# Moving the seam between two instruction orders from word 571 to word 1042

## The chip, the cores and the metric

The kernel runs on one core of a Trainium2 chip. The metric is device time in microseconds, from one launch to its end; a run is told by its time, and a change by the medians of runs of both kernels on the same chip. The engines go by the short names of the profile: PE is TensorE (PEld its weight loads), DVE is VectorE, ACT is ScalarE, POOL is GpSimd and SP is SyncE, which issues most of the DMAs.

## The reference

Two blocks follow each other. The first is a linear attention with a complex, data-dependent decay (batch 4, 8 heads, 768 positions, head size 48). The second is a feed-forward block with three up-projections, of which the maximum is taken, and one down-projection.

```python
mag = np.sqrt(a_re * a_re + a_im * a_im)
scale = np.minimum(mag, 0.999) / (mag + 1e-06)
a_re_n, a_im_n = (a_re * scale, a_im * scale)
for t in range(S):                                  # S_re, S_im start at zero
    ar, ai = (a_re_n[:, :, t, :, None], a_im_n[:, :, t, :, None])
    new_re = ar * S_re - ai * S_im
    new_im = ar * S_im + ai * S_re
    kv = np.einsum('bhd,bhe->bhde', k[:, :, t], v[:, :, t])
    S_re, S_im = (new_re + kv, new_im)
    y[:, :, t] = np.einsum('bhd,bhde->bhe', q[:, :, t], S_re)
x = y.transpose(0, 2, 1, 3).reshape(3072, 384)
h = np.maximum(np.maximum(x @ w1, x @ w2), x @ w3)  # w1, w2, w3: 384 x 768
out = h @ w_out                                     # w_out: 768 x 384
```

All tensors are float32.

## The kernel before

The positions are cut into 24 tiles of 128 (4 batch rows of 6 tiles). Two tiles, called x and y, of two batch rows make one group, and there are 12 groups, 0 to 11. The work of a group is cut into some hundred and fifty short steps. Each step has a name and a group number, and such a pair is called a word: `Fy:6` is step `F` of tile y in group 6. The string `SCHEDULE` lists 1,880 words in one order, written out in full, and the kernel runs through it and emits each word's instructions. A small class wraps each engine and chains its instructions, so each engine runs its own words strictly in the order of the list; across engines the tile framework puts semaphores where data or buffers demand it.

```python
def g(*a, **kw):
    ins = f(*a, **kw)
    if self.last is not None:
        tc.add_manual_dep(ins.ins, self.last.ins.name, order, reason="the schedule's order")
```

The order in `SCHEDULE` is put together from two orders: words up to a seam come from one, and the rest, those not used yet, from the other, in its sequence. The seam stands at word 571.

Two more tables go with the list. `SLOTS` gives, for each PSUM tile in the order of its first use, one of four slots named 0, 2, 4 and 6, of two banks each; a tile has to wait until the last reader of the slot's tile before is done. `OTHER` names the words that run on the engine that is not their usual one: copies (`Kc`, `Qc`, `x`), magnitudes (`abs`, `af`) and maxima (`relu`, `u01`, `u11`) go from ACT to DVE, and the additions `Lnop` and `addw` go from a DMA issued by POOL to DVE.

```python
def banks(nm, n=None):
    ps = psum.tile([P, 2, 512], FP, tag="ps" + next(slots), name=nm)

def activation(func, **kw):
    need = SETS.get(func, T.get("set"))
    if need != T.get("set"):
        act.preload_act_table_set(need)
        T["set"] = need
    act.activation(func=func, **kw)
```

ACT has two sets of function tables, one for Ln and Exp and one for Sin and Arctan. `activation` puts a table load into ACT's queue whenever the set changes from one word to the next; copies, Relu, Abs and Square run with either set.

The words that matter below, with the engine of each:

- Gates, one word a group: `sqr`, `sqi`, `lnL`, `expw`, `expe`, `lne`, `relu`, `abs`, `lnw`, `expL`, `atan` on ACT, `add`, `xor`, `half`, `mulai`, `mulw`, `stt`, `turn` on DVE; `Lnop` and `addw` add by DMA. They turn `a_re`, `a_im` into a log magnitude `Ln` and an angle `w` (`expL` is an Exp, `atan` an Arctan).
- Angles, one word a tile: `cs` sums the angles on PE, `t` (ACT) and `nf` (DVE) take off whole turns, `Cd` carries the last angle into the next group's `ar` by two DMAs that POOL issues and that add, `sa` and `sb` are the Sin words on ACT.
- Decays: `sums` and `F` on PE; `En`, `Ek`, `Eq` and `f0` to `f3` are Exp words on ACT.
- Keys and queries: `mk`, `mq`, `uk`, `uq`, `kEn`, `Q1`, `Q2`, `KB`, `QB`, `QG` on DVE; `tpk`, `tpq` transpose on PE, `Kc`, `Qc` copy the result out of PSUM.
- Scores and state: `A`, `B`, `dk`, `y` on PE; `g0` to `g3` and `h0` to `h3` on DVE, `b0`, `b1` on ACT; `x` copies `y` out of PSUM into the features (`xy:5` is that copy for tile y of group 5).
- Feed-forward: `U01`, `U02`, `U11`, `U12` (nine products of 128 rows each) on PE, and `u` of the same number takes the maximum (`u01`, `u11` on ACT, `u02`, `u12` on DVE). The down-projection is done by Strassen's scheme: sums `S1` to `S4` on DVE, products `P1` to `P7`, `Px`, `Py` on PE, results `r1`, `r6`, `r75`, `r57`, `ox`, `oy` on ACT and DVE. `Dx`, `Dy` write the output.
- Loads: `Lr`, `Li`, `Lk`, `Lq`, `Lv`, all issued by SP.

PE works on pieces of its array that differ in shape. `U`, `P` use 128*128 (rows * columns), `A`, `B`, `y` 128*32, `cs` 128*64, `tpk`, `tpq` 64*128 and `sums`, `F`, `dk` 64*64. A tile change is two words in turn on PE with different shapes. All lines of the profile name line 201, the wrapper, so groups of instructions are told apart by tile.

Of the kernel before, what the change touches and what calls it, by code (L numbers as in the profile page):

```python
# [54 lines left out]
Cdy:3 Lkx:4 f1x:4 f0x:4 U01:2 uqy:3 f3x:4 mulw:4 stt:4 atan:4 tpky:3 Kcy:3 Ax:3 g0x:3 mqx:4 g1x:3 Bx:3 g2x:3 g3x:3 b1x:3
b0x:3 u01:2 Cdx:3 turn:4 U02:2 Lrx:5 u02:2 mkx:4 kEny:3 csy:4 csx:4 tx:4 nfx:4 ty:4 nfy:4 yx:3 xx:3 sumsy:4 KBy:3 Eqy:4
Eky:4 Lry:5 S3:2 Eny:4 sqr:5 dky:3 h1y:3 h2y:3 h3y:3 tpqy:3 Qcy:3 Q2y:3 Lix:5 sqi:5 Px:2 afy:4 add:5 lnL:5 expe:5 Dy:1
U12:2 u12:2 S1:2 Py:2 P7:2 Q1y:3 relu:5 lne:5 QBy:3 afx:4 P4:2 Ay:3 By:3 expw:5 S2:2 g0y:3 sbx:4 abs:5 g1y:3 sax:4 QGy:3
ukx:4 uqx:4 P6:2 P5:2 S4:2 g2y:3 g3y:3 P2:2 P1:2 Lqy:4 r1:2 Liy:6 mqy:4 b1y:3 P3:2 b0y:3 r6:2 r75:2 tpkx:4 r57:2 ox:2
# [5 lines left out]
sumsy:5 h1y:4 h2y:4 tx:5 nfx:5 h3y:4 afy:5 yx:4 Eky:5 Eny:5 Eqy:5 afx:5 Q2y:4 Q1y:4 sbx:5 P5:3 P1:3 P7:3 Lky:5 sax:5
Ay:4 xx:4 KBy:4 ukx:5 uqx:5 Lrx:7 tpqx:5 S2:3 expw:6 relu:6 QBy:4 Lnop:6 mky:5 tpkx:5 S4:3 Kcx:5 g0y:4 Qcx:5 P6:3 Px:3
Py:3 r1:3 By:4 P2:3 P4:3 say:5 sby:5 QGy:4 g1y:4 abs:6 g2y:4 g3y:4 b1y:4 b0y:4 KBx:5 mqy:5 r6:3 r75:3 r57:3 kEnx:5 oy:3
Q1x:5 uky:5 xor:6 Lry:7 sqr:7 Fy:5 f2y:5 sumsx:6 uqy:5 f3y:5 yy:4 P3:3 ox:3 f0y:5 Lkx:6 xy:4 QGx:5 addw:6 U11:4 Liy:7
Dx:3 QBx:5 Ekx:6 mkx:6 Enx:6 Lvx:5 f1y:5 lnw:6 Lqx:6 h0y:5 u11:4 Q2x:5 expL:6 mulai:6 mulw:6 U01:4 u01:4 tpky:5 h0x:5
# [10 lines left out]
tx:7 afy:7 yx:6 xx:6 Ay:6 S1:5 dky:6 h1y:6 nfx:7 h2y:6 h3y:6 Px:5 Py:5 abs:8 addw:8 half:8 g0y:6 g1y:6 say:7 KBy:6 sby:7  # L80
Lqy:7 P1:5 r1:5 g2y:6 afx:7 S2:5 P2:5 P7:5 sbx:7 sax:7 QBy:6 P5:5 lnw:8 ukx:7 S4:5 g3y:6 P6:5 mqy:7 r6:5 uqx:7 Lqx:8
QGy:6 P3:5 By:6 P4:5 r75:5 r57:5 tpkx:7 oy:5 ox:5 b0y:6 kEnx:7 mky:7 uky:7 b1y:6 tpqx:7 yy:6 Kcx:7 uqy:7 xy:6 expL:8
mulw:8 sumsx:8 Qcx:7 Eqx:8 mulai:8 mqx:8 Q1x:7 Ekx:8 Lkx:8 mkx:8 Fy:7 f1y:7 f0y:7 f3y:7 Enx:8 f2y:7 QGx:7 U01:6 Lvx:7
QBx:7 Q2x:7 u01:6 U11:6 Cdy:7 Liy:9 u11:6 Lvy:8 tpky:7 kEny:7 h0x:7 tpqy:7 Kcy:7 h0y:7 dkx:7 Qcy:7 sumsy:8 Fx:8 Eky:8
Eqy:8 h1x:7 Eny:8 h2x:7 KBx:7 f2x:8 f0x:8 h3x:7 Q2y:7 stt:8 Dx:5 f1x:8 atan:8 Cdx:7 turn:8 Lix:9 Lrx:9 Ax:7 g0x:7 g1x:7
Lry:9 sqr:9 Dy:5 g2x:7 sqi:9 add:9 f3x:8 lnL:9 expe:9 U12:6 lne:9 u12:6 Lvy:7 g3x:7 U02:6 u02:6 S3:6 Bx:7 b0x:7 b1x:7
dky:7 S1:6 h1y:7 h2y:7 csx:8 csy:8 tx:8 ty:8 nfy:8 h3y:7 afy:8 yx:7 xx:7 P7:6 relu:9 expw:9 KBy:7 say:8 sby:8 Lqy:8 P1:6
S2:6 P6:6 nfx:8 Q1y:7 QBy:7 Lky:8 mky:8 By:7 afx:8 uky:8 sbx:8 Ay:7 abs:9 Lnop:9 tpky:8 Lrx:10 QGy:7 g0y:7 g1y:7 g2y:7
sax:8 Kcy:8 P5:6 S4:6 g3y:7 ukx:8 r1:6 uqx:8 mqy:8 r6:6 h0x:8 b0y:7 r75:6 r57:6 b1y:7 Px:6 P2:6 P3:6 Py:6 P4:6 kEny:8
tpkx:8 ox:6 oy:6 addw:9 lnw:9 tpqx:8 yy:7 Qcx:8 sumsx:9 Kcx:8 kEnx:8 xy:7 Fy:8 Q1x:8 sumsy:9 Enx:9 xor:9 f1y:8 f0y:8  # L90
expL:9 half:9 mulai:9 Cdy:8 f2y:8 f3y:8 Eny:9 Liy:10 mulw:9 QGx:8 stt:9 U11:7 KBx:8 Eky:9 uqy:8 Lry:10 sqr:10 Lqx:9
Ekx:9 Lix:10 Lvx:8 sqi:10 Lkx:9 mkx:9 Eqx:9 QBx:8 u11:7 mqx:9 Q2x:8 U01:7 Cdx:8 atan:9 u01:7 add:10 lnL:10 Eqy:9 expe:10
U02:7 turn:9 tpqy:8 Qcy:8 dkx:8 relu:10 u02:7 h1x:8 Fx:9 Dy:6 h2x:8 Dx:6 f1x:9 f0x:9 Ax:8 h3x:8 Bx:8 g0x:8 g1x:8 U12:7
g2x:8 g3x:8 lne:10 Q2y:8 f3x:9 b0x:8 f2x:9 h0x:9 Lqy:9 Q1y:8 csy:9 ty:9 u12:7 S3:7 csx:9 nfy:9 expw:10 tx:9 b1x:8 S1:7
P1:7 r1:7 QBy:8 S2:7 nfx:9 KBy:8 sbx:9 afy:9 Ay:8 g0y:8 g1y:8 afx:9 g2y:8 g3y:8 Lky:9 yx:8 xx:8 sax:9 say:9 ukx:9 abs:10
By:8 h0y:8 sby:9 mky:9 P6:7 uqx:9 P7:7 mqy:9 P5:7 r6:7 S4:7 Py:7 b0y:8 Px:7 r75:7 r57:7 QGy:8 P4:7 oy:7 tpqx:9 tpkx:9
Lnop:10 Kcx:9 b1y:8 sumsx:10 kEnx:9 Qcx:9 Q1x:9 dky:8 h1y:8 h2y:8 h3y:8 Enx:10 uky:9 addw:10 lnw:10 Lkx:10 P2:7 expL:10
P3:7 Ekx:10 ox:7 KBx:9 yy:8 xy:8 Fy:9 f0y:9 f1y:9 QGx:9 f2y:9 Lvx:9 f3y:9 dkx:9 Eqx:10 QBx:9 U01:8 mkx:10 u01:8 Q2x:9
Ax:9 xor:10 half:10 h1x:9 Lvy:9 Bx:9 uqy:9 h2x:9 h3x:9 U11:8 g0x:9 Liy:11 g1x:9 Dy:7 g2x:9 g3x:9 Lqx:10 mqx:10 Cdy:9
u11:8 Fx:10 b0x:9 b1x:9 tpky:9 tpqy:9 kEny:9 Lry:11 mulw:10 mulai:10 stt:10 Dx:7 f1x:10 f3x:10 Qcy:9 Kcy:9 Q2y:9 U02:8  # L100
u02:8 f2x:10 U12:8 Lrx:11 sqr:11 Cdx:9 S3:8 atan:10 turn:10 f0x:10 Lix:11 yx:9 sqi:11 add:11 lnL:11 xx:9 expe:11 csy:10
xor:11 ty:10 csx:10 u12:8 S1:8 KBy:9 sumsy:10 nfy:10 Eny:10 Eky:10 S2:8 Q1y:9 QBy:9 afy:10 Eqy:10 Lqy:10 dky:9 P5:8
tx:10 lne:11 P6:8 P7:8 Ay:9 h0y:9 nfx:10 h1y:9 By:9 QGy:9 h2y:9 h3y:9 g0y:9 sbx:10 g1y:9 g2y:9 relu:11 afx:10 sax:10
ukx:10 g3y:9 P1:8 S4:8 r1:8 say:10 sby:10 mqy:10 r6:8 r75:8 b0y:9 b1y:9 expw:11 Py:8 P4:8 r57:8 Px:8 uqx:10 yy:9 xy:9
# [938 lines left out]
```

## Time and profile before

| What | Value |
|---|---|
| Time, median of 3 runs | 558.26 us (557.66 to 558.30) |
| The profiled execution | 555.38 us, its span 553.6 us |
| Granted PE clock, mean | 0.991 |
| Busy: PE, DVE, ACT, POOL | 525.3, 482.6, 365.0, 71.8 us |
| ACT table loads | 47, 1283 ns each |
| DMA | 47.90 MB, mean 87 GB/s |

The span goes from the first to the last instruction of the profiled execution; the time of that execution is 1.8 us longer. Busy times are unions over the span; PE's matmuls overlap each other, so a matmul's own duration (382 ns for the largest group) is longer than the time that one adds (the 792 of that group are busy for 177.4 us). From 110 to 495 us PE is busy at least 99% of every 55 us, and the first 55 us hold 35.75 us of PE work.

### The profile page before, as it was taken

The page shows a single profiled execution, that of the slowest core. Times are in us where ns is not written, and L with a number is a line of the kernel's source. Part 1 is how long each engine was busy: PE and PEld are TensorE (multiplying, and loading weights), DVE is VectorE, ACT ScalarE, POOL GpSimd, SP SyncE. Part 2 cuts the span into 40 slices and gives each one's busy share as a digit, 9 for nine tenths or more (in the row PEclk, how much of TensorE's full clock was granted, in tenths as well). Part 3 has the DMA queues.
Part 4 walks back from the last instruction along what each step waited for, and adds up shares of the span by engine and source line. Part 5 has one row for each costly group of instructions (what it writes and reads, how often), then busy time and mean ns, then how long its engine had stood idle before and what let it go on. Part 6 is the DMA issues. An engine that isn't in the chain of part 4 may idle for free.

```text
span 553.6 us, 22691 instructions
## 1 busy us (share of the span) xinstructions
PE 525.3 (95%) x10086; PEld 449.6 (81%) x10086; DVE 482.6 (87%) x752; ACT 365.0 (66%) x650; POOL 71.8 (13%) x114
## 2 busy tenths in 40 slices
...
GB/s 217 295 247 176 157 136 79 48 128 77 2 117 103 59 118 73 61 50 84 95 96 58 37 100 119 75 92 49 69 122 17 32 110 68 2 31 2 31 1 28
DMA packets 142097, 47.90 MB, mean 87 GB/s; under 512 B 130480, under 2 KB 135600, under 8 KB 142000
## 3 DMA queue, kind: packets, MB, share of 16 engines
...
q8 instruction: 79, 1.29, 1.0%
q14 instruction: 18, 0.15, 0.1%
...
## 4 chain that ended last, share of the span: by engine, by line
PE 84%; DVE 7%; ACT 4%; issue 2%; SPq 2%; DMA 1%; DVEq 0%; ACTq 0%
PE up L201 33%; PE op L201 24%; PE y L201 7%; PE A L201 5%; PE tp L201 4%; PE dk L201 3%; PE cs L201 3%; PE sums L201 2%; DVE w L201 2%; SPq L201 2%; PE F L201 2%; PE B L201 1%; DVE atm L201 1%; DMA wo<-in_moe_w_dram 1%; DVE uk L201 1%
## 5 line engine op out<-in xcount | busy, mean ns | idle before, releaser
L201 PE MATMUL up<-xhx,w 128*128 128x256 f32 x792 | 177.4, 382 | 0.2
L201 PEld LDWEIGHTS up<-xhx,w 128*128 128x128 f32 x792 | 148.6, 190 | 21.9 <-issue 0.3
L201 ACT ACT_TABLE_LOAD x47 | 60.3, 1283 | 1.6 <-PEq L1027 0.8
L201 PE MATMUL op<-wo,xhx 128*128 128x192 f32 (+1 forms) x220 | 48.3, 363 | 0.5 <-DVE uk L201 0.5
L201 ACT COPY atm<-B 32x128 f32<-32x128 f32 x96 | 24.6, 256 | 35.1 <-DVE atm L201 21.6
L201 DVE TENSOR_TENSOR Q<-Q,f 112x1024 f32<-112x1024 f32 (+1 forms) x48 | 45.3, 951 | 0.9 <-ACT f L201 0.3
L201 ACT ACTIVATE f<-F 48x232 f32<-48x232 f32 x96 | 34.5, 359 | 14.3 <-PE F L201 6.9
L201 POOL DMA_DIRECT2D ar<-nf x40 | 34.6, 1304 | 58.7 <-DVE ar L201 53.1
L201 PEld LDWEIGHTS op<-wo,xhx 128*128 128x128 f32 x220 | 36.6, 190 | 4.7 <-issue 1.0
L201 PE MATMUL y<-atm,vb 128*32 128x64 f32 x1152 | 39.1, 222 | 0.1
L201 POOL DMA_DIRECT2D Ln<-e x10 | 9.2, 923 | 228.6 <-ACT e L201 71.0
L201 PE MATMUL y<-QG,g 112*32 112x64 f32 x1408 | 37.8, 219 | 0.2 <-issue 0.2
L201 PEld LDWEIGHTS y<-atm,vb 128*32 128x32 f32 x1152 | 32.3, 110 | 4.7 <-issue 2.7
L201 DVE TENSOR_TENSOR ot<-ot,op 128x384 f32<-128x384 f32 (+1 forms) x56 | 25.4, 465 | 11.8 <-PE op L201 7.3
L201 PEld LDWEIGHTS y<-QG,g 112*32 112x32 f32 x1408 | 34.8, 110 | 0.3 <-issue 0.3
L201 PE MATMUL op<-wo,strassen 128*128 128x192 f32 x176 | 33.0, 331 | 0.0
L201 DVE COPY_PREDICATED atm<-masko,A 128x256 f32<-128x256 uint8 x72 | 31.2, 434 | 1.7
L201 PE MATMUL op<-w,strassen 128*128 128x192 f32 x176 | 32.4, 329 | 0.0
L201 PE MATMUL A<-Q,K 112*32 112x80 f32 x1536 | 31.6, 234 | 0.2 <-DVE Q L201 0.2
L201 ACT COPY ot<-op 128x192 f32<-128x192 f32 (+1 forms) x13 | 4.5, 344 | 40.4 <-PE op L201 40.4
L201 ACT COPY Q<-tp 112x1024 f32<-112x1024 f32 x22 | 22.3, 1014 | 11.4 <-PE tp L201 11.3
L201 DVE TENSOR_TENSOR xhx<-xhx,up 128x768 f32<-128x768 f32 x22 | 20.8, 952 | 10.3 <-PE up L201 9.0
...
## 6 DMA issues: line engine op xcount, KB each, us to landing
...
```

The costliest lines, as they stand in the source:

```text
L201: ins = f(*a, **kw)
```

## The change

The seam moves from word 571 to word 1042: more words come from the first order, fewer from the second. The list keeps its 1,880 words. The first 571 stay, those from word 1071 on stay, and the 500 between stand in another sequence. The first order is told to have 189 tile changes, and the new list has 192. `SLOTS` changes from the 88th tile on, and `OTHER` loses `Kcy:3 xy:3 relu:5 afx:5 u01:4 afy:6` and gains `Lnop:4 u01:2 afy:4 Qcx:4 u11:3 u01:3 Kcy:4 xy:4 u11:4 xx:5 Lnop:7`. No function changes. The diff, with parts of the list left out:

```diff
--- before.py
+++ after.py
@@ SCHEDULE
 Cdy:2 Cdx:2 sumsy:3 Bx:2 u01:1 Ay:2 Fx:3 KBy:2 g0y:2 g1y:2 h0y:2 b0x:2 b1x:2 Eny:3 g2y:2 stt:3 Eqy:3 sqr:4 atan:3 g3y:2
...
-By:2 Ekx:3 P5:1 P6:1 P1:1 P7:1 sax:3 sbx:3 Lqy:3 Lqx:3 abs:4 mqx:3 afy:3 b0y:2 b1y:2 say:3 Lky:3 Lkx:3 mkx:3 Dy:0 h0x:3
-sby:3 J4:0 Px:1 P2:1 ukx:3 tpkx:3 lne:4 Lnop:4 r1:1 Liy:5 mky:3 S4:1 Kcx:3 uqx:3 yy:2 Lqx:4 kEnx:3 mqy:3 tpqx:3 Qcx:3
-P3:1 r6:1 xy:2 Py:1 r75:1 P4:1 Fy:3 uky:3 r57:1 f0y:3 f1y:3 half:4 oy:1 ox:1 Q1x:3 addw:4 dkx:3 h1x:3 Lvy:3 f2y:3 f3y:3
...
-oy:2 kEnx:4 tpqx:4 yy:3 xy:3 Fy:4 say:4 Lky:4 sby:4 mky:4 uky:4 Lnop:5 Kcx:4 uqy:4 sumsx:5 xor:5 half:5 U11:3 KBx:4
...
-lne:6 b1x:4 tpky:4 turn:5 mqx:5 b0x:4 tpqy:4 Qcy:4 u12:3 Lvy:4 kEny:4 S1:3 csy:5 ty:5 csx:5 Kcy:4 dky:4 nfy:5 S3:3
...
-expw:7 afy:6 P7:4 abs:7 Lky:6 Ay:5 QBy:5 g0y:5 g1y:5 g2y:5 yx:5 g3y:5 addw:7 sbx:6 sax:6 ukx:6 uqx:6 By:5 say:6 P5:4
-xx:5 P6:4 r1:4 r6:4 lnw:7 xor:7 S4:4 half:7 Px:4 P2:4 b0y:5 Py:4 r75:4 P4:4 r57:4 P3:4 expL:7 mulw:7 QGy:5 oy:4 tpqx:6
-tpkx:6 b1y:5 Lnop:7 mky:6 Qcx:6 Q1x:6 ox:4 Liy:8 kEnx:6 yy:5 sumsx:7 xy:5 Cdx:6 Enx:7 Fy:6 f2y:6 f0y:6 f3y:6 mulai:7
-f1y:6 Eqx:7 QBx:6 QGx:6 Q2x:6 stt:7 Lqx:7 Ekx:7 Lix:8 U01:5 sqi:8 Lry:8 Cdy:6 Kcx:6 Lrx:8 Lvx:6 dkx:6 h1x:6 sby:6 mqx:7
...
+By:2 Ekx:3 P5:1 P6:1 P1:1 P7:1 sax:3 sbx:3 Lqy:3 Lqx:3 abs:4 mqx:3 afy:3 b0y:2 b1y:2 say:3 r1:1 sby:3 addw:4 lne:4 Lix:5
+Dy:0 Lry:5 Lkx:3 Lvx:4 Px:1 P2:1 S4:1 mkx:3 P3:1 Py:1 J4:0 yy:2 xy:2 r6:1 r75:1 uqx:3 ukx:3 Lky:3 mqy:3 uqy:3 r57:1
+mky:3 tpkx:3 tpqy:3 tpqx:3 Lrx:5 Lvy:3 Liy:5 h0x:3 Kcx:3 kEnx:3 P4:1 Qcy:3 lnw:4 Qcx:3 uky:3 dkx:3 Fy:3 U11:2 f1y:3
...
+g1x:3 afx:4 U12:2 u12:2 g2x:3 g3x:3 S1:2 Fx:4 f2x:4 f3x:4 f1x:4 f0x:4 sumsy:4 Eny:4 Eqy:4 Eky:4 Lkx:4 dky:3 Lvy:4 Liy:6
...
+mkx:4 ukx:4 P7:2 P6:2 P5:2 P1:2 yx:3 Ay:3 xx:3 lnw:5 lne:5 expL:5 r1:2 Enx:4 Px:2 Py:2 P4:2 QGy:3 S4:2 r6:2 g0y:3 g1y:3
+g2y:3 g3y:3 afy:4 mulw:5 r75:2 half:5 P2:2 By:3 P3:2 b1y:3 b0y:3 yy:3 say:4 xy:3 r57:2 mqx:4 uqx:4 ox:2 mulai:5 tpqx:4
+Qcx:4 stt:5 Lnop:5 Cdx:4 Cdy:4 tpkx:4 sqr:6 atan:5 sqi:6 Kcx:4 U01:3 uky:4 turn:5 oy:2 kEnx:4 u01:3 csx:5 add:6 Fy:4
...
+u12:3 tpqy:4 tpky:4 Qcy:4 csy:5 ty:5 expw:6 relu:6 abs:6 U02:3 nfx:5 Kcy:4 Q1y:4 Q2y:4 Ay:4 Ax:4 nfy:5 kEny:4 QBx:4
...
+mkx:5 mulw:6 QGy:4 r75:3 r57:3 Fx:5 sbx:5 sby:5 f2x:5 f3x:5 h1y:4 stt:6 oy:3 yy:4 xy:4 mqx:5 say:5 atan:6 sax:5 P3:3
...
+nfx:6 tpqy:5 Fy:5 U12:4 f3y:5 Qcy:5 f0y:5 f1y:5 f2y:5 ty:6 KBx:5 QBx:5 add:7 Q1y:5 Q2y:5 dkx:5 sumsy:6 afx:6 nfy:6 h1x:5
+lnL:7 expw:7 expe:7 Bx:5 u12:4 Ay:5 g0y:5 b0x:5 b1x:5 yx:5 Eky:6 relu:7 afy:6 mqx:6 g1y:5 xx:5 sbx:6 sax:6 h0y:5 S1:4
...
+P3:4 b0y:5 b1y:5 f0x:6 tpqx:6 Qcx:6 expL:7 Lqy:6 mqy:6 say:6 mulw:7 oy:4 tpkx:6 Q1x:6 ox:4 kEnx:6 yy:5 sumsx:7 xy:5
+Enx:7 Fy:6 f2y:6 f0y:6 f3y:6 mulai:7 f1y:6 Eqx:7 QBx:6 QGx:6 Q2x:6 stt:7 Lqx:7 Ekx:7 U01:5 sqi:8 Kcx:6 dkx:6 h1x:6 sby:6
...
@@ SLOTS, OTHER
-0240624024202406402024604642064262624062046420640426240260620406404624624620620260264062624062426020
-4242046062620460264260460240260264460266062460406246046026402426402464026402640624240206062460264264
-2064022640406204026402642604620420620406402626462042606426602640406260460626046264206040624046404664
-0464
+0240624024202406402024604642064262624062046420640426240260620406404624624620620260264064262464046042
+0624060202264264020240246206426264004206404602464204606240024046042060426042604620204246462064260260
+2460422604046240426042602640624024624046042626062402646026642604046264064626406260246404620406040660
+4060
-Zf:0 Zg:0 afx:0 relu:1 Qcy:0 addw:2 Lnop:2 Wg8:0 u21y:0 addw:3 relu:4 afx:3 abs:4 Kcy:3 xx:3 relu:5 xy:3 afx:5 addw:6
-u01:4 afx:6 afy:6 abs:7 relu:8 Kcy:6 afy:7 afx:7 relu:9 abs:9 u11:7 u01:7 afx:9 Kcx:9 xy:8 u11:8 Kcy:9 afy:10 abs:11
-Kcx:10 Qcy:10 Kcy:11 Kcx:11 xy:11 u01:11 u11:11
+Zf:0 Zg:0 afx:0 relu:1 Qcy:0 addw:2 Lnop:2 Wg8:0 u21y:0 addw:3 relu:4 afx:3 abs:4 Lnop:4 u01:2 xx:3 afy:4 Qcx:4 u11:3
+u01:3 Kcy:4 xy:4 addw:6 u11:4 afx:6 abs:7 xx:5 Lnop:7 relu:8 Kcy:6 afy:7 afx:7 relu:9 abs:9 u11:7 u01:7 afx:9 Kcx:9 xy:8
+u11:8 Kcy:9 afy:10 abs:11 Kcx:10 Qcy:10 Kcy:11 Kcx:11 xy:11 u01:11 u11:11
```

More of the change, by code (lines that the diff above doesn't have):

```diff
@@ L55 @@
[L55 to L59, printed above, removed]
@@ L65 @@
[L65 to L69, printed above, removed]
@@ L80 @@
[L80 to L104, printed above, removed]
@@ new lines @@
+sumsy:5 Eky:5 Dy:2 Lvy:5 Lqy:5 Lry:7 Lrx:7 Lqx:5 Lky:5 Lkx:5 Lvx:5 Dx:2 sumsx:5 yx:4 Eqy:5 afx:5 Eny:5 By:4 P7:3 P6:3
+Ekx:5 Eqx:5 lnw:6 Enx:5 xx:4 b0y:4 expL:6 S4:3 xor:6 Lnop:6 h0y:4 r1:3 b1y:4 Px:3 Py:3 P2:3 P4:3 dky:4 r6:3 mulai:6
+mkx:5 mulw:6 QGy:4 r75:3 r57:3 Fx:5 sbx:5 sby:5 f2x:5 f3x:5 h1y:4 stt:6 oy:3 yy:4 xy:4 mqx:5 say:5 atan:6 sax:5 P3:3
+mky:5 half:6 uqx:5 turn:6 mqy:5 f1x:5 f0x:5 U01:4 u01:4 h2y:4 h3y:4 uky:5 ox:3 uqy:5 ukx:5 U02:4 u02:4 S3:4 tpqx:5
+tpky:5 tpkx:5 kEnx:5 h0x:5 Kcy:5 Qcx:5 Q1x:5 QGx:5 Q2x:5 kEny:5 sumsx:6 U11:4 u11:4 Lix:7 Lix:8 Lrx:8 Lvx:6 Lry:8 Liy:7
@@ new lines @@
+expw:8 tx:7 afy:7 yx:6 xx:6 Ay:6 S1:5 dky:6 h1y:6 nfx:7 h2y:6 h3y:6 Px:5 Py:5 abs:8 addw:8 half:8 g0y:6 g1y:6 say:7
+KBy:6 sby:7 Lqy:7 P1:5 r1:5 g2y:6 afx:7 S2:5 P2:5 P7:5 sbx:7 sax:7 QBy:6 P5:5 lnw:8 ukx:7 S4:5 g3y:6 P6:5 mqy:7 r6:5
+uqx:7 Lqx:8 QGy:6 P3:5 By:6 P4:5 r75:5 r57:5 tpkx:7 oy:5 ox:5 b0y:6 kEnx:7 mky:7 uky:7 b1y:6 tpqx:7 yy:6 Kcx:7 uqy:7
+xy:6 expL:8 mulw:8 sumsx:8 Qcx:7 Eqx:8 mulai:8 mqx:8 Q1x:7 Ekx:8 Lkx:8 mkx:8 Fy:7 f1y:7 f0y:7 f3y:7 Enx:8 f2y:7 QGx:7
+U01:6 Lvx:7 QBx:7 Q2x:7 u01:6 U11:6 Cdy:7 Liy:9 u11:6 Lvy:8 tpky:7 kEny:7 h0x:7 tpqy:7 Kcy:7 h0y:7 dkx:7 Qcy:7 sumsy:8
```

44 lines of the change are left out of this document (33 added, 11 removed).

## The prediction

> **What bounds the kernel now.** I read the page first: its busy shares and the chain that ended last.
>
> ```profile
> span 553.6 us, 22691 instructions
> PE 525.3 (95%) x10086; PEld 449.6 (81%) x10086; DVE 482.6 (87%) x752; ACT 365.0 (66%) x650; POOL 71.8 (13%) x114
> ...
> PE 84%; DVE 7%; ACT 4%; issue 2%; SPq 2%; DMA 1%; DVEq 0%; ACTq 0%
> L201 DVE TENSOR_TENSOR xhx<-xhx,up 128x768 f32<-128x768 f32 x22 | 20.8, 952 | 10.3 <-PE up L201 9.0
> ```
>
> TensorE carries 84% of the chain and is busy 95% of the span. The profiled execution took 555.38 us: the span of 553.6 and 1.8 around it. The median of the three timed runs is 558.26, 2.88 above that execution, so I work out a difference against the profiled run and add it to the median. A measurement of this kernel can tell about 0.2% from no change, 1.1 us here.
>
> Second view: the busy time by stage, for the stretch that the changed words fill. In the old list it runs from `Px:1` (the first matrix word there) to the start of `dkx:6`.
>
> ```profile
> core 0: us, PE busy (x) PEld busy (x) DVE busy (x) ACT busy (x) POOL busy (x), PEclk, DMA share, GB/s
> 148.01:284.58 136.57, 136.37 (x2732) 119.78 (x2730) 126.90 (x195) 101.00 (x173) 15.92 (x19) 1.00 0.44 84
> ```
>
> TensorE is idle for 0.2 us of 136.57 and its clock is full, so there is nearly nothing to win in the stretch. A busy TensorE can still stretch, so I went to the timeline, where the time from a word's first matmul to the next word's first matmul is the word's real length.
>
> ```profile
> 199.05 11.92 PE L201 MATMUL up<-xhx,w 128*128 128x256 f32 x54
> 210.90 1.08 PE L201 MATMUL dk<-vb,uk 64*64 64x48 f32 x62
> ...
> 276.58 0.66 PE L201 MATMUL tp<-ident,uq 64*112 64x64 f32 x16
> 277.08 0.61 PE L201 MATMUL tp<-ident,uk 64*112 64x64 f32 x16
> 277.62 0.32 PE L201 MATMUL y<-atm,vb 128*32 128x64 f32 x8
> ...
> 280.05 0.52 PE L201 MATMUL F<-cuts,Ln 64*48 64x29 f32 x32
> 280.50 4.15 PE L201 MATMUL up<-xhx,w 128*128 128x256 f32 x18
> 284.58 1.14 PE L201 MATMUL dk<-vb,uk 64*64 64x48 f32 x64
> 285.65 1.31 PE L201 MATMUL A<-Q,K 112*32 112x80 f32 x64
> ```
>
> Words of one kind repeat to within some hundredths of a us. Three `U` words (54 matmuls) take 210.90 - 199.05 = 11.85; one alone between other shapes takes 284.58 - 280.50 = 4.08. So two take 7.77, one 3.885, and entering and leaving the 128*128 shape once costs 0.20. Added up in this way, each kind at its undisturbed length with its shape changes, the 104 matrix words between 148.01 and 284.58 need 135.6. So the old stretch loses 0.95 in all (an estimate; the idle time above bounds it at 0.2 from below). Of that I can put about 0.5 to named hand-overs, in which a matrix word starts only a twentieth to a fifth of a us after the copy that it waits for.
>
> **The change part by part.** Work is neither added nor taken away: the same 1,880 words stand in the list, and those before the old word 571 and from word 1071 keep their places. PSUM slots after the stretch are the old ones with 0 and 4 exchanged.
>
> Shape changes. I counted them in the two lists: 189 before, 192 now, all three new ones in the stretch (49 to 52), with two more returns to 128*128 (15 to 17). Two returns cost 2 x 0.20. The third change I put at 0.1, half a return. Together +0.5, between 0.3 (three at the 0.1 of half a return) and 0.6 (three at 0.2). The Trainium skill, TensorEngine Tiling (Array Packing), section Key Properties, says that changing the tiling mode drains TensorE. By that rule a change would cost what is still in the array at it, here 0.07 to 0.16 (4.15 less 4.08 for a `U` word, 0.66 less 0.50 for a transpose); three would be +0.2 to +0.5 and the whole sum +1.8 to +2.1, so the measured 0.20 for going in and out is near its upper end.
>
> Engines. By `OTHER`, eleven copies, maxima and additions go to VectorE in the stretch and six leave it.
>
> ```profile
> L201 DVE COPY K<-tp 112x1024 f32<-112x1024 f32 x7 | 8.6, 1222 | 1.7 <-PE tp L201 1.6
> ```
>
> The copies `Kcy:4`, `Qcx:4` at 1.22 each and six words of the 0.95 size (`u01:2`, `u01:3`, `u11:3`, `u11:4`, and `Lnop:4`, `Lnop:7`, which were DMA additions) come; one copy, one 0.95 and four small ones go. The net is five more words, about +5.5 of work. VectorE had 136.57 - 126.90 = 9.7 idle in the stretch, so about 4 is left. That is enough on the average, so I price nothing for it; it is why hand-overs get tighter (below). ScalarE gets some 2 us less work and still 15 table loads in the stretch, but they stand elsewhere.
>
> The seam. This is the largest term. In the new list the words from 1042 on go back to the other order, and just ahead of it stand `tpqx:6 Qcx:6 expL:7 Lqy:6 mqy:6 say:6 mulw:7 oy:4 tpkx:6 Q1x:6 ox:4 kEnx:6 yy:5 sumsx:7 xy:5 Enx:7 Fy:6`. `expL:7` is an Exp, `say:6` a Sin, `Enx:7` an Exp: two table loads now stand between `Qcx:6` and `Enx:7`. In the old list `expL:7` and `say:6` came earlier, and ScalarE had time to spare here, as its own timeline shows:
>
> ```profile
> 271.50 0.32 ACT L201 COPY ot<-op 128x192 f32<-128x192 f32 x1 [2.58 <-PE op L201]
> 271.84 1.28 ACT L201 ACT_TABLE_LOAD   x1
> 273.13 0.84 ACT L201 ACTIVATE L<-w 128x768 f32<-128x768 f32 x1
> ...
> 274.30 0.84 ACT L201 ACTIVATE L<-L 128x768 f32<-128x768 f32 x1
> 275.16 0.53 ACT L201 COPY atm<-B 32x128 f32<-32x128 f32 x2
> 277.28 1.01 ACT L201 COPY Q<-tp 112x1024 f32<-112x1024 f32 x1 [1.60 <-PE tp L201]
> 279.48 0.48 ACT L201 COPY xhx<-y 128x384 f32<-128x384 f32 x1 [1.18 <-PE y L201]
> 280.45 0.49 ACT L201 ACTIVATE En<-sums 128x384 f32<-128x384 f32 x1 [0.49 <-DVE uk L201]
> 280.95 1.47 ACT L201 ACTIVATE f<-F 48x232 f32<-48x232 f32 x4
> 282.44 0.49 ACT L201 ACTIVATE Eq<-sums 128x384 f32<-128x384 f32 x1
> 282.82 0.48 ACT L201 ACTIVATE Ek<-sums 128x384 f32<-128x384 f32 x1
> ...
> 283.93 1.01 ACT L201 COPY K<-tp 112x1024 f32<-112x1024 f32 x1
> ```
>
> Count from the start of `tpqx:6`, 276.58 in the old run. `Qcx:6` starts 0.70 later (277.28), since it waits for that transpose. Then the new queue: `Qcx:6` about 0.90 to the next start (1.01 less the overlap of 0.1 that two neighbours show, as Eq to Ek 0.38 for a 0.49), so `expL:7` at 1.60; 0.85 (274.30 to 275.16) to the load at 2.45; 1.29 (271.84 to 273.13) to `say:6` at 3.74; 0.38 for a 128x384 activation (282.44 to 282.82) to `xy:5` at 4.12. In the old run `Fy:6` started 280.05 - 279.48 = 0.57 after `xy:5` did; it takes the PSUM slot that `xy:5` empties, and by the new `SLOTS` it still does. So `Fy:6` can start at 4.69. Undisturbed TensorE is there at 280.05 - 276.58 = 3.47: a wait of 1.2.
>
> The same queue then makes `Ax:6` late, which needs `Kcx:6`. After `xy:5` comes the second load: `Enx:7` at 4.12 + 0.38 + 1.29 = 5.79. It also waits for `kEnx:6` on VectorE, whose queue hangs on `expL:7`:
>
> ```profile
> 278.33 0.69 DVE L201 TENSOR_TENSOR Q<-Q,f 112x512 f32<-112x512 f32 x1
> 278.94 0.55 DVE L201 TENSOR_TENSOR ot<-ot,op 128x384 f32<-128x384 f32 x1
> 279.40 0.95 DVE L201 TENSOR_TENSOR uk<-uk,En 128x768 f32<-128x768 f32 x1
> 280.27 0.95 DVE L201 TENSOR_TENSOR ai<-ai,L 128x768 f32<-128x768 f32 x1
> ```
>
> `mulw:7` at 2.47, 0.87 for its size (279.40 to 280.27), `oy:4` 0.46 (278.94 to 279.40), `Q1x:6` 0.61, `ox:4` 0.46, `kEnx:6` 0.95: done at 5.82, so `Enx:7` at 5.85. From the start of `Enx:7` to the end of `Kcx:6` the old run took 284.94 - 280.45 = 4.49, and the words in it are the same: 10.34, and `Ax:6` not before 10.4 to 10.5. Undisturbed TensorE is there at 285.65 - 276.58 = 9.07. So TensorE stands 1.3 to 1.5 behind after the seam, 1.2 of it at `Fy:6` and the rest at `Ax:6`. I take +1.5, bounds 1.2 (the first wait alone) and 1.6. Queued behind the waiting `Fy:6` are `U01:5`, `dkx:6` and everything that follows.
>
> Other hand-overs. Ahead of the seam I compared, for each matrix word of the new list, the sum of matrix words with the sum of ScalarE and VectorE words since the last matrix word that these wait for. Four come out late: `U11:2` after `Qcx:3` (under 0.1), `P7:2` after `Eky:4` (0.25: four `f` words, then three exponentials, for four matrix words), `csy:5` after `u12:3` (0.95 for the maximum, 0.1 to 0.2 of hand-over, against 0.50 + 0.54 for two transposes: 0.1), `Ay:5` after `h1x:5` (0.25). Together +0.6, bounds 0.2 and 1.6; the upper one holds two that I put at nothing: `yy:4` after `h1y:4` (up to 0.4, covered as long as `yy:4`'s first matmuls use no state) and `csx:5` (below). Against this the old 0.5 of named hand-overs goes away, bounds 0.2 and 0.95.
>
> Sum: 0.5 + 1.5 + 0.6 - 0.5 = +2.1, bounds 0.3 + 1.2 + 0.2 - 0.95 = +0.75 and 0.6 + 1.6 + 1.6 - 0.2 = +3.6. The profiled run would be 557.5, the median 560.4.
>
> **The rivals.** Given back later (not slower). From word 1071 on both lists are alike, and the old run loses some 1.4 us there in waits of TensorE. If what those waits hang on is finished at a time of its own, a TensorE that comes 2.1 late finds it done, and 0.7 is left: 559.0, within 0.2%. It decides where the waits end on DMA or on work queued long before. For: VectorE has idle time with which to get ahead. Against: the largest of these, 0.6 between `dky:8` and `P2:7`, stands in the chain that ended last, and that chain goes through the copy of a transpose:
>
> ```profile
> 397.68 1.23 DVE K L201
> ```
>
> TensorE had made that transpose just before, so the copy moves along with a later TensorE. Chance 0.12.
>
> The carry (slower than the forecast). `Cdx:4` and `Cdy:4` add the carried angle into the next group's `ar` by four GpSimd DMAs after `half:5`, and `turn:5` and `csx:5` wait for them.
>
> ```profile
> 202.73 3.29 POOL L201 DMA_DIRECT2D ar<-nf  x4 [12.84 <-DVE ar L201]
> DMA to landing us min/median/max: 2.1/3.9/6.6
> ```
>
> The four take 3.29 on the queue; the last starts about 1.6 after the first (half of it, an estimate) and lands 2.1 to 6.6 later, so 3.7 to 8.2 after `half:5`. In the new list `half:5` ends some 0.7 ahead of `yy:3` by the sums of VectorE and TensorE words up to there, and up to `csx:5` TensorE then has `yy:3` (1.7 of the 2.43 from 277.62 to 280.05), two transposes (1.04) and a `U` word (4.0); less 0.87 for `turn:5` and 0.15 of hand-over that leaves about 6.3 for the DMAs. At the median landing, 5.5, they are in time; at the worst they cost 1.9, on top of the 2.1 less the 0.3 of neighbouring hand-overs that this wait would cover: 562.0. Chance 0.15.
>
> Dearer table loads (slower than the forecast). If ScalarE stood still around each of the two loads for as long as the load itself, the seam would cost 2 x 1.28 more: 563.0. The rows speak against it: the copy ahead of the load ended at 271.82, the load began at 271.84, and the next word began 0.01 after its end. Chance 0.02. The Trainium skill, ScalarE: Activation LUTs, section What ACT_TABLE_LOAD costs, counts a drain of 1.38 us beside a load of 1.28 for each switch. By that the time would be 563.2, an estimate; this trace shows the load's 1.28 and no such drain.
>
> Better fed (faster). If the new order loses nothing anywhere in the stretch, it is 0.5 - 0.95 = -0.45: 557.8, still within 0.2%. Faster by more needs a gain in the common part. Chance 0.05.
>
> **How the numbers follow.** My forecast of the seam wait has 0.66, and its own range is 559.0 to 561.9. With the carry and the drain, slower by over 0.2% has 0.83; within 0.2% has 0.12, the giving back; faster 0.05. The range for 8 in 10 runs from 558.8, just under the giving back, to 562.2, just over the worst of the carry.
>
> **What would show it.** Right: `Fy:6` starts about 1.2 later after `tpqx:6` than the old 3.47, the table load stands between `expL` and the sine there, and the TensorE words from `Px:1` to `dkx:6` take about 138.5. Wrong: the stretch at or under 136.6, or the stretch longer and the span not, which would be time given back after 290.

## The result, and the profile after

| | before | after |
|---|---|---|
| Median of the timed runs (22 each, same chip) | 556.42 us | 559.92 us |
| Profiled execution, its span | 555.38, 553.6 us | 559.5, 557.4 us |
| Start of `Px:1`, of `dkx:6`, of `Ax:6` | 148.01, 284.58, 285.65 | 149.49, 288.89, 290.12 |
| Start of `dky:8`, of `P3:7` | 398.30, 401.26 | 402.73, 405.21 |

The kernel after is slower, by a ratio of 1.0063 with an interval of 1.0044 to 1.0082: 3.5 us of 556.4, between 2.4 and 4.6. The forecast was +2.1, with bounds of +0.75 and +3.6. The predicted median of 560.4 came closer than that, since the kernel before itself ran 1.8 lower here than in the runs from which I predicted.

The page of the kernel after, its span and busy shares:

```profile
span 557.4 us, 22673 instructions
...
PE 527.4 (95%) x10086; PEld 450.2 (81%) x10086; DVE 486.5 (87%) x757; ACT 362.2 (65%) x647; POOL 69.8 (13%) x112
```

TensorE is busy 2.1 longer and the span is 3.8 longer. The busy time by stage of the kernel after, from `Px:1` to `dkx:6` (columns as in the prediction):

```profile
149.49:288.89 139.40, 137.60 (x2731) 119.07 (x2731) 130.09 (x200) 97.40 (x169) 13.67 (x17) 1.00 0.37 72
```

The stretch grew from 136.57 to 139.40, and TensorE's idle time in it from 0.20 to 1.80. Up to `Ax:6`, which also waits, it grew from 137.64 to 140.64, +3.0. The clock is full in both, so this is time lost in the list, and the timeline shows where. TensorE of the kernel after at the seam:

```profile
279.61 0.66 PE L201 MATMUL tp<-ident,uq 64*112 64x64 f32 x16
...
284.32 0.56 PE L201 MATMUL F<-cuts,Ln 64*48 64x29 f32 x32 [1.07 <-ACT xhx L201]
284.81 4.15 PE L201 MATMUL up<-xhx,w 128*128 128x256 f32 x18
288.89 1.14 PE L201 MATMUL dk<-vb,uk 64*64 64x48 f32 x64
290.12 1.11 PE L201 MATMUL A<-Q,K 112*32 112x80 f32 x52
```

And ScalarE of the kernel after, in the same time:

```profile
280.31 1.02 ACT L201 COPY Q<-tp 112x1024 f32<-112x1024 f32 x1 [0.78 <-PE tp L201]
281.22 0.85 ACT L201 ACTIVATE L<-L 128x768 f32<-128x768 f32 x1
282.08 1.28 ACT L201 ACT_TABLE_LOAD   x1
283.38 0.52 ACT L201 ACTIVATE CS<-t 128x384 f32<-128x384 f32 x1
283.81 0.46 ACT L201 COPY xhx<-y 128x384 f32<-128x384 f32 x1
284.28 1.28 ACT L201 ACT_TABLE_LOAD   x1
285.58 0.49 ACT L201 ACTIVATE En<-sums 128x384 f32<-128x384 f32 x1
...
289.05 1.02 ACT L201 COPY K<-tp 112x1024 f32<-112x1024 f32 x1
```

This is the predicted queue: `Qcx:6`, the Exp `expL:7`, a load, the Sin `say:6`, then `xy:5` at 283.81, and `Fy:6` behind it. `Fy:6` starts 284.32 - 279.61 = 4.71 after `tpqx:6` (forecast 4.69, before 3.47), and `Ax:6` 10.51 after it (forecast 10.4 to 10.5).

From here on a loss is the time from one word's first matmul to the next word's, less the length that such a word has where nothing holds it; where the next word starts late, the loss goes by the late word's name. By this measure the old stretch up to `Ax:6` loses 0.95 and the new one 3.46, and shape changes add 0.48: the 3.0. The 3.46 are `Fy:6` 1.25, `Ax:6` 0.16, `Fy:5` 0.47, a gap inside `yy:3` 0.46, `sumsx:5` 0.27, `tpkx:3` 0.17, and small ones. After the stretch 0.65 comes back, most of it between `dky:8` and `P3:7` (2.96 before, 2.48 after). So the profiled execution is 2.35 longer from `Px:1` on. The rest of its 3.8, 1.5, lies ahead of `Px:1`, where TensorE has the same words in both.

### The profile page after: what moved, and what is told of

It is laid out like the page before. It is cut to its first block, busy times and chain, and to the rows that moved or that the text cites. A ratio compares the mean times of both kernels' runs of the same rounds, so it can differ in the third digit from the quotient of the medians.

```text
span 557.4 us, 22673 instructions
## 1 busy us (share of the span) xinstructions
PE 527.4 (95%) x10086; PEld 450.2 (81%) x10086; DVE 486.5 (87%) x757; ACT 362.2 (65%) x647; POOL 69.8 (13%) x112
## 4 chain that ended last, share of the span: by engine, by line
PE 82%; DVE 7%; ACT 7%; issue 1%; DMA 1%; SPq 0%; DVEq 0%; ACTq 0%
PE up L201 31%; PE op L201 23%; PE y L201 7%; PE A L201 4%; PE dk L201 3%; PE tp L201 3%; PE sums L201 2%; PE wm L201 2%; PE cs L201 2%; DVE atm L201 2%; PE F L201 2%; ACT L L201 1%; PE B L201 1%; PE pw L201 1%; DVE Q L201 1%
## 5 line engine op out<-in xcount | busy, mean ns | idle before, releaser
L201 PEld LDWEIGHTS A<-Q,K 112*32 112x32 f32 x1536 | 27.3, 110 | 4.5 <-issue 3.3
L201 POOL DMA_DIRECT2D Ln<-e x8 | 7.1, 893 | 181.2 <-ACT e L201 73.2
L201 PEld LDWEIGHTS op<-wo,strassen 128*128 128x128 f32 x176 | 28.9, 190 | 1.0
```

## The experiments

My theory: the words that the seam brings together make ScalarE's queue late (`Fy:6`, `Ax:6`), shape changes cost 0.5, and other hand-overs the rest. The rivals are the fuller VectorE, another price of a shape change, and something equally late behind each wait.

**The kernel after, again.**

> The changed kernel as it is, for the runs beside it. Theory (the seam): time some 1.006 of the kernel before; in its profile Fy:6 waits 1.2 to 1.3 us for xy:5, and the stretch from Px:1 to Ax:6 is 3.0 us longer than before. Rival (start-up): the first 148 us were 1.5 us longer in the changed kernel's profile although the list is the same there; if that is the cause, it shows again here, and if it is the spread of the runs, it differs from run to run.

Measured: 560.15 us, ratio 1.0061 (1.0034 to 1.0088). `Fy:6` loses 1.25, `Ax:6` 0.16, `sumsx:5` 0.26, `Fy:5` 0.44: data waits repeat within 0.03. The gap inside `yy:3` doesn't: 0.74. `Px:1` starts at 149.57, so the late start shows again in this execution; what the other kernels say of it stands at the end of the next section.

**The sine away from the seam.**

```diff
-sax:6 h0y:5
+sax:6 say:6 h0y:5
-Lqy:6 mqy:6 say:6 mulw:7
+Lqy:6 mqy:6 mulw:7
```

> The changed kernel with the one word say:6 moved up, directly behind sax:6, so that it shares that word's table set and two table loads (of 46 switches) fall away. Theory (the seam wait is ScalarE's queue with two table loads in it): the wait at Fy:6 goes from 1.25 to under 0.2 us, that at Ax:6 from 0.16 to nothing, the stretch is 1.2 to 1.5 us shorter than in the changed kernel, ratio to the kernel before about 1.003 to 1.004. Rival (VectorE's load makes the seam late): the wait at Fy:6 stays over 1 us.

Measured: 559.74 us, ratio 1.0037 (1.0018 to 1.0056; it overlaps the interval of the kernel after). `Fy:6` no longer waits, yet `Px:1` to `Ax:6` takes 140.90, no less than the 140.64. TensorE (`U01:5`), and then VectorE, of this kernel:

```profile
285.13 4.15 PE L201 MATMUL up<-xhx,w 128*128 128x256 f32 x18 [1.05 <-DVE ot L201]
```

```profile
282.59 0.96 DVE L201 TENSOR_TENSOR w<-w,L 128x768 f32<-128x768 f32 x1 [0.68 <-ACT L L201]
283.46 0.55 DVE L201 TENSOR_TENSOR ot<-ot,op 128x384 f32<-128x384 f32 x1
...
284.53 0.55 DVE L201 TENSOR_TENSOR ot<-ot,op 128x384 f32<-128x384 f32 x1
```

`U01:5` now waits 1.1 for the PSUM slot that `ox:4` empties (284.53 + 0.55 = 285.08). `ox:4` stands in VectorE's order behind `mulw:7`, which idles 0.68 for the Exp. So two queues hang on the place of `expL:7`, equally late, and taking away one wait uncovers the other.

**The Exp alone, and both** (the Exp goes ahead of `Qcx:6`; "both" is in the two mended kernels further down).

```diff
-f0x:6 tpqx:6 Qcx:6 expL:7
+f0x:6 expL:7 tpqx:6 Qcx:6
```

> The kernel after, with expL:7 alone moved, behind f0x:6 (ahead of Qcx:6 on ScalarE); the sine stays. Theory of the two queues: VectorE's queue is then early, U01:5 does not wait; ScalarE's queue is shorter by one Exp (0.85), so Fy:6 still waits 0.3 to 0.5 instead of 1.25, and Ax:6 about 0.16. Rival (the sine and its two loads alone make the wait): Fy:6 waits 1.1 or more, as in the kernel after.

Measured: 560.59 us in its one run, which can't be told from the kernel after. `Fy:6` in its trace:

```profile
285.47 0.56 PE L201 MATMUL F<-cuts,Ln 64*48 64x29 f32 x32 [0.33 <-ACT xhx L201]
```

Here `Fy:6` loses 0.51 instead of 1.25, `Ax:6` 0.17, and `U01:5` doesn't wait. This is the theory's side, just over its 0.3 to 0.5. With neither word moved the seam loses 1.41, with the sine alone 1.41 (1.11 and 0.30), with the Exp alone 0.68.

**The seam's words in the old list.** The kernel before, with only these words brought together:

```diff
-P3:4 expL:7 mulw:7 QGy:5 oy:4 tpqx:6
+P3:4 QGy:5 tpqx:6
-mky:6 Qcx:6 Q1x:6
+mky:6 Qcx:6 expL:7 say:6 mulw:7 oy:4 Q1x:6
```

(`say:6` also leaves its place behind `By:5`.)

> The kernel before, with the Exp and the Sin brought to where the kernel after has them: expL:7, say:6, mulw:7 and oy:4 directly behind Qcx:6. Everything else, the shape changes and the engines too, is as before. Theory (the seam's wait comes from these words' place alone): Fy:6 waits 1.1 to 1.4, Ax:6 0.1 to 0.4, dkx:6 and the end come 1.2 to 1.6 later: Px:1 to Ax:6 takes 139.0 to 139.4 instead of 137.6, ratio 1.002 to 1.003. Rival (it needs the new order's fuller engines): under 0.5 in all, ratio 1.000 to 1.001.

Measured: 558.63 us, ratio 1.0024 (1.0000 to 1.0048). TensorE of this kernel (`tpqx:6`, `Fy:6`, `Ax:6`):

```profile
280.76 0.66 PE L201 MATMUL tp<-ident,uq 64*112 64x64 f32 x16
...
285.47 0.56 PE L201 MATMUL F<-cuts,Ln 64*48 64x29 f32 x32 [1.07 <-ACT xhx L201]
...
291.29 0.41 PE L201 MATMUL A<-Q,K 112*32 112x80 f32 x12
```

`Fy:6` starts 4.71 after `tpqx:6`, to the hundredth as in the kernel after, and loses 1.25; `Ax:6` loses 0.17. The stretch takes 139.58, over the forecast by a gap of 0.5 inside `yx:3` that hangs on nothing in the trace. So these four words' places are enough for the seam's wait; neither the new order nor the fuller engines are needed. It is the trace that shows this: the timed runs fit it, but their interval begins at 1.0000.

**The new order with the old division of engines.** `OTHER` is that of before.

> The changed kernel with the kernel before's OTHER: the 17 words are back on their old engines, the order and the slots are the new ones. Theory (VectorE's five more words tighten hand-overs): the waits at Fy:5 behind g3x:5 (0.48 us) and at sumsx:5 behind g3y:4 (0.27 us) go, 0.6 to 0.8 us less; the 1.25 us at Fy:6 stay. Rival (the order alone makes them): they stay, and ScalarE, which takes 2.6 us more, adds waits of its own, so the stretch is no shorter.

Measured: 574.19 us, ratio 1.0314 (1.0282 to 1.0345). New waits come in the stretch, the longest of them at `Ax:5`:

```profile
PE A L201 <- ACT En L201: 3.7, 1, 3.7
```

The loss at `Fy:5` all but goes, but with TensorE held up by 3.7 at `Ax:5` just before, that says nothing of its cause. The loss at `sumsx:5` stays. `sumsy:5` and `sumsx:5` in the kernel after:

```profile
225.41 0.56 PE L201 MATMUL sums<-Ln,mid 64*64 64x192 f32 x8
...
226.37 0.56 PE L201 MATMUL sums<-Ln,mid 64*64 64x192 f32 x8
```

And in this run, with `g3y:4` on VectorE:

```profile
233.76 0.56 PE L201 MATMUL sums<-Ln,mid 64*64 64x192 f32 x8
...
234.72 0.56 PE L201 MATMUL sums<-Ln,mid 64*64 64x192 f32 x8
```

```profile
234.24 0.42 DVE L201 COPY_PREDICATED atm<-masko,A 128x256 f32<-128x256 uint8 x1
```

`sumsx:5` starts 0.96 after `sumsy:5` in both, here too right behind the end of `g3y:4` (234.24 + 0.42 = 234.66), with five words fewer on VectorE. So this wait is not the fuller VectorE's, against the theory. Beyond that the run doesn't tell what the fuller VectorE costs, since it changes too much at once.

**The price of a shape change.** The kernel before, with twelve products each moved behind the next matrix word; 189 changes become 209.

> The kernel before with twelve product words (P or Px) each moved behind the next matrix word of another shape: twelve more returns to 128*128, 209 tile changes in place of 189, nothing else. Theory (a return costs 0.2 us, and leaving another shape once more 0.05 to 0.2): TensorE's words grow by 2.4 to 3.4 us, ratio about 1.005. Rival (shape changes hide in the overlap of neighbouring matmuls): under 0.5 us, ratio 1.000.

Measured: 570.97 us, ratio 1.0251 (1.0226 to 1.0276). TensorE before, and in this kernel, from the start of `P1:3` to that of `tpqx:5` (between them stand `P7:3` and `Ay:4`, and in the changed list `Ay:4` and `P7:3`):

```profile
225.49 1.46 PE L201 MATMUL op<-wo,xhx 128*128 128x192 f32 x8
...
229.43 0.38 PE L201 MATMUL tp<-ident,uq 64*112 64x64 f32 x6
```

```profile
226.35 1.46 PE L201 MATMUL op<-wo,xhx 128*128 128x192 f32 x8
...
230.49 0.38 PE L201 MATMUL tp<-ident,uq 64*112 64x64 f32 x6
```

The same three words take 229.43 - 225.49 = 3.94 and 230.49 - 226.35 = 4.14: a return to 128*128 costs 0.20, as the prediction had it, and 0.29 at another place, where it splits two transposes. The total missed the expectation by far. The moved products hold PSUM slots and results back: new waits of 1.0 to 1.8 stand at five words, one of which (1.82 inside a `y` word) the trace puts down to nothing.

**VectorE's load: one maximum back on ScalarE.** In the kernel after, `u11:4` leaves `OTHER`.

> The kernel after, with one maximum (u11:4, 0.95 us) back on ScalarE, which is idle there; the list is the same. Theory (the five more words on VectorE are not free): VectorE reaches g0x:5 to g3x:5 0.87 sooner, so the wait of 0.47 at Fy:5, which starts 0.15 after g3x:5, is gone, while those at sumsx:5 (0.27) and Fy:6 (1.25) stay; Px:1 to Ax:6 takes 140.1 to 140.4. Rival (VectorE's load costs nothing; the gap at Fy:5 has another cause): Fy:5 still waits 0.4 or more.

```profile
256.84 1.58 PE L201 MATMUL A<-Q,K 112*32 112x80 f32 x64 [3.68 <-ACT En L201]
258.36 2.83 PE L201 MATMUL cs<-w,upto 128*64 128x192 f32 x16
```

562.63 us in its one run. I had overlooked what stands behind `u11:4` on ScalarE: it waits for `U11:4` there, and behind it stand the copy and the exponentials without which `Ax:5` can't start. `Fy:5` no longer waits, but only because these come first; that says nothing of its cause.

**The same without that trap.** `u11:4` stands behind `Enx:6` on ScalarE, and `KBy:4` behind `g3y:4` on VectorE.

```diff
-U11:4 u11:4 Lix:7
+U11:4 Lix:7
-Enx:6 Ax:5
+Enx:6 u11:4 Ax:5
-g2y:4 KBy:4 g3y:4
+g2y:4 g3y:4 KBy:4
```

> The kernel after, with two words of VectorE touched: u11:4 goes to ScalarE and stands behind Enx:6, so that the exponentials that held up Ax:5 in the run before do not stand behind it; and KBy:4 (0.6) goes behind g3y:4. Theory: Ax:5 does not wait; sumsx:5, which starts 0.05 after g3y:4, does not wait any more (0.27 before), so that wait was VectorE's load; Fy:5 still waits 0.4 to 0.5, because g0x:5 to g3x:5 (2.2) follow the scores of Ax:5 1.38 after its start whatever VectorE did before, and only csx:6, csy:6 and tpqy:5 (2.5) stand between: that wait is the order's. Rival (VectorE's fuller queue makes both): neither waits. Px:1 to Ax:6 140.3 by the theory, 139.9 by the rival.

560.8 us. TensorE and VectorE of the kernel after around `Fy:5`:

```profile
254.75 1.31 PE L201 MATMUL A<-Q,K 112*32 112x80 f32 x64
255.99 1.52 PE L201 MATMUL cs<-w,upto 128*64 128x192 f32 x16
257.44 0.66 PE L201 MATMUL tp<-ident,uq 64*112 64x64 f32 x16
258.45 0.56 PE L201 MATMUL F<-cuts,Ln 64*48 64x29 f32 x32 [0.35 <-DVE atm L201]
```

```profile
255.22 0.95 DVE L201 TENSOR_SCALAR xhx<-up 128x768 f32<-128x768 f32 x1
256.13 0.73 DVE L201 COPY_PREDICATED atm<-maskd,A 128x512 f32<-128x512 uint8 x1
256.90 1.41 DVE L201 COPY_PREDICATED atm<-masko,A 128x256 f32<-128x256 uint8 x3
```

And of this kernel, without `u11:4` on VectorE:

```profile
256.16 1.31 PE L201 MATMUL A<-Q,K 112*32 112x80 f32 x64
...
259.84 0.56 PE L201 MATMUL F<-cuts,Ln 64*48 64x29 f32 x32 [0.32 <-DVE atm L201]
```

```profile
257.54 0.73 DVE L201 COPY_PREDICATED atm<-maskd,A 128x512 f32<-128x512 uint8 x1 [0.82 <-PE A L201]
```

`g0x:5` starts 1.38 after `Ax:5` in both: the maximum ended just when the scores were ready, and with it gone VectorE idles 0.82. `Fy:5` still loses 0.44. So this wait is the order's: too few matrix words between the scores and the word that takes their PSUM slot. So is the one at `sumsx:5`: with `KBy:4` behind `g3y:4` it starts 0.71 after `sumsy:5`, and the 0.27 is gone. `KBy:4` runs on VectorE in the kernel before as well, and without the five more words the wait stayed (the run with the old division). The stretch takes 141.17 all the same, since the gap inside `yy:3` is 1.23 in this run; the forecast of 140.3 fails on that.

**The tail, in the kernel before.**

```diff
-P7:11 r75:11 ox:11 P4:11
+P7:11 P4:11 r75:11 ox:11
```

> The kernel before, with one word of its last group moved: P4:11 ahead of r75:11 and ox:11, so that the last product need not wait 1.4 for a PSUM slot that ox:11 empties. The seam is the old one. Theory (that wait stands in the chain that ended last): TensorE ends about 1.4 sooner, and the span is 0.5 to 1.4 shorter: ratio 0.9975 to 0.999. Rival (the end hangs on the last copies and on the output's DMA): TensorE ends sooner and the span stays, 1.000 within 0.001.

Measured: 555.91 us, ratio 0.9993 (0.9972 to 1.0015). `P4:11` loses 1.40 in the kernels that keep its place and nothing in this one, and from `Px:1` to the end the span is 405.1 instead of 405.6. The last row of VectorE shows where the rest went: four sums of results now stand in a line at the end, up to after the last product.

```profile
546.93 1.46 PE L201 MATMUL op<-w,xhx 128*128 128x192 f32 x8
...
548.43 1.47 DVE L201 TENSOR_TENSOR ot<-ot,op 128x384 f32<-128x384 f32 x4 [0.75 <-PE op L201]
```

Too little to be told from no change by the timed runs.

**Mending the kernel after.** Three kernels. The first moves `expL:7` far up, behind `lnw:7`, and `say:6` behind `sax:6`; the second adds `u11:4` on ScalarE and the tail; the third takes the places that the other runs bear out: `expL:7` behind `f0x:6`, `say:6` behind `sax:6`, `KBy:4` behind `g3y:4`, the tail.

> The kernel after, with two words moved in the list: expL:7 directly behind lnw:7, and say:6 directly behind sax:6. Both queues that hang on ScalarE at the seam are then free of the Exp and the Sin. Theory (two equally late queues: ScalarE's Qcx:6, expL:7, load, say:6, xy:5 for Fy:6, and VectorE's mulw:7, oy:4, Q1x:6, ox:4 behind expL:7 for U01:5): the waits at Fy:6 (1.25), U01:5 and Ax:6 (0.16) are all under 0.2, Px:1 to Ax:6 takes 139.1 to 139.4 instead of 140.6 to 140.9, and the ratio to the kernel before falls from 1.006 to about 1.0035. Rival (a third queue is late as well, or TensorE gives the time up elsewhere, as when the sine alone was moved): the stretch stays at 140.5 or more and the ratio at 1.005 or more.

Measured: 559.41 us, ratio 1.0041 (1.0022 to 1.0060). Its profiled execution took 1828.30 us, so only the timed runs are used, and they don't tell the theory from the rival. The second kernel has the same seam and a trace.

> The three edits together on the kernel after: expL:7 and say:6 moved up, u11:4 on ScalarE, and P4:11 ahead of r75:11. Theory (each takes away its own wait and they add up): against the kernel after -1.4 at the seam, -0.5 at Fy:5 and -1 at the end, so about +0.6 us against the kernel before: ratio 1.000 to 1.002. Rival (the waits move on to the next late thing): 1.003 or more.

Measured: 563.68 us, ratio 1.0126 (1.0090 to 1.0162): the trap at `Ax:5` again (3.75). At the seam the waits of `Fy:6` and `U01:5` are gone, but `tpqx:6` now loses 0.47 behind `b1y:5`, which stands behind the moved Exp on ScalarE.

> The kernel after, with the mends that the runs so far bear out: expL:7 behind f0x:6, say:6 behind sax:6, KBy:4 behind g3y:4, P4:11 ahead of r75:11. Theory (each wait goes and nothing new comes): -1.4 at the seam, -0.27 at sumsx:5, -0.5 at the end: Px:1 to Ax:6 takes 138.8 to 139.3, and the ratio to the kernel before falls from 1.006 to 1.002 (1.001 to 1.003). Rival (something equally late stands behind each): 1.004 or more.

Measured: 557.34 us, ratio 1.0003 (0.9976 to 1.0030). The stretch up to `Ax:6`, and TensorE at the seam:

```profile
148.89:288.11 139.22, 138.28 (x2796) 120.19 (x2795) 131.09 (x200) 96.21 (x169) 13.67 (x17) 1.00 0.39 74
```

```profile
281.84 0.53 PE L201 MATMUL F<-cuts,Ln 64*48 64x29 f32 x32
282.65 4.15 PE L201 MATMUL up<-xhx,w 128*128 128x256 f32 x18 [0.28 <-DVE ot L201]
```

`Fy:6` doesn't wait; `U01:5` loses 0.35 and `Ax:6` 0.30, so 0.65 of the seam's 1.41 is left. `sumsx:5` and `P4:11` don't wait. Four moved words bring the slow kernel back to the time of the kernel before, within its interval. They don't undo the whole change: the stretch up to `Ax:6` is still 1.6 longer than the 137.64 of the kernel before, and the fourth word, in the tail, took 0.5 off the span of the kernel before as well. From `Px:1` to the end the span is 405.85 against 405.6. No kernel here is shown to beat the kernel before.

## Why the prediction came out as it did

**Direction and largest single term: right, and shown.** The seam was to cost 1.5 and costs 1.41 (1.25 and 0.16), by the queue and the start times that were worked out, and the old list shows the same 1.25 when the words are moved there. One half was overlooked: the prediction worked out VectorE's queue for `kEnx:6`, but not that `ox:4` in it holds the slot of `U01:5`. That was hidden behind the first wait and didn't change the sum; it would have misled anyone who mended only the sine.

**Shape changes: right.** +0.5 forecast; 0.48 by the word lengths, and 0.20 for a return where one was added on purpose.

**"I price nothing for it", of VectorE's five more words: no cost is shown.** The average idle time was there (130.09 busy of 139.40 after). The two waits behind VectorE, at `Fy:5` and `sumsx:5`, are the order's: the first stays without `u11:4`, the second stays with the old division of engines. No run isolates what the five words cost.

**Other hand-overs: the term that was mis-sized.** +0.6 was forecast at four named places; these came to about 0.2 (`U11:2` 0.09, `P7:2` 0.03, `csy:5` 0.08, `Ay:5` 0). In their stead stand `Fy:5` 0.47, `sumsx:5` 0.27, `tpkx:3` 0.17 and the gap in `yy:3` 0.46: about 1.6 in all, at the upper bound and more than the seam. `Fy:5` could have been found in the list: the scores' 1.38, the 2.2 of `g0x:5` to `g3x:5` and 0.15 of hand-over together 3.7, stand against the 3.2 that `Ax:5`, `csx:6`, `csy:6` and `tpqy:5` take, as the rows above show. The comparison went from wait to wait and not by PSUM slots. The gap in `yy:3` could not have been found there. This is why the stretch took 139.4 and not 138.5.

**Old hand-overs gone, -0.5:** right. Of the 3.46, some 0.5 stands at none of the places named here, against 0.95 before.

**The sum: near in part by luck.** Up to `Ax:6` it is 1.4 + 0.5 + 1.6 - 0.5 = 3.0 against +2.1. From `Px:1` to the end the profiles give 2.35, because 0.65 came back that the sum had at nothing.

**Given back later (0.12).** It was not the outcome: of the predicted 1.4 only 0.65 came back, and not shown to be by that way. The prediction held that the wait between `dky:8` and `P2:7` would move along with TensorE, because of the copy ahead of it. The rows of `dky:8` and `P2:7` in the kernel before, in the kernel after, and in the old list with the seam's words moved show that the wait shrinks:

```profile
398.30 1.14 PE L201 MATMUL dk<-vb,uk 64*64 64x48 f32 x64
399.96 1.46 PE L201 MATMUL op<-wo,xhx 128*128 128x192 f32 x8 [0.53 <-DVE uk L201]
```

```profile
402.73 1.14 PE L201 MATMUL dk<-vb,uk 64*64 64x48 f32 x64
403.80 1.57 PE L201 MATMUL op<-wo,xhx 128*128 128x192 f32 x8
```

```profile
403.93 1.14 PE L201 MATMUL dk<-vb,uk 64*64 64x48 f32 x64
405.35 1.46 PE L201 MATMUL op<-wo,xhx 128*128 128x192 f32 x8 [0.28 <-issue]
```

The loss is 0.12 to 0.66 in the four kernels with the old list and 0.03 in those with the new one. The copy did move along: it starts 0.62 ahead of `dky:8` in the kernel before (the prediction's 397.68) and 0.61 ahead of it after (402.12). So the wait doesn't hang on the copy, although the first fence names the VectorE word behind it; the last fence puts it down to "issue", to nothing that the profile shows. From word 1071 on the two lists differ only in the names of two PSUM slots. The cause stays open.

**The carry (0.15):** didn't occur; `csx:5` doesn't wait in the kernel after. (The terms given for the time that the DMAs have add up to 6.4, not 6.3, so the worst would cost 1.8.) **Dearer table loads (0.02):** not seen. `expL:7` ends at 282.07, the load starts at 282.08 and the sine 0.02 after the load's end. The Trainium skill, ScalarE: Activation LUTs, section What ACT_TABLE_LOAD costs, counts a drain of 1.38 beside each load; no gap of that kind stands in these rows. **Better fed (0.05):** no; the stretch loses more.

**What stays open.** By the profiles the change costs 2.3 to 2.6 from `Px:1` on (spans of 557.4 and 557.8 less 149.49 and 149.57, against 405.6); the timed runs say 3.5, between 2.4 and 4.6. If there is a remainder it lies ahead of `Px:1`. `Px:1` starts between 147.2 and 151.7 in the four old-list kernels profiled and between 148.1 and 151.0 in the new-list ones, so one profile each can't say whether the head differs. The means are 148.7 of four and 149.7 of nine, with a spread inside each group that is larger than the difference.
